# Windowed attention and a convolution gate: a woven order of work, two-bank and one-bank PSUM buffers, weights loaded later, half-size angle tables

## The chip, the core and the metric

The kernel runs on one core of a Trainium2 chip. The time is that of one execution on the device, in microseconds (us). TensorE (PE) has two clock levels, 1.2 and 2.4 GHz; the profile prints the granted clock as a share of the higher one, so 1.00 is 2.4 GHz and 0.50 is 1.2 GHz. DVE is VectorE, ACT is ScalarE, POOL is GpSimd, and SP issues most of the transfers (SPq is its queue of instructions).

## What is computed

The inputs are `q`, `k`, `v` of shape (4, 8, 768, 64), a flag per head, and the three weights of a gate, of shapes (512, 1536), (768, 512) and (512, 512). Of the reference, cut to what matters:

```python
scores = scale * np.matmul(q, k.transpose(0, 1, 3, 2))
stream_keep = causal & (is_sink | in_win)        # 4 sink keys, a window of 64
mask = np.where(retr, causal, stream_keep)       # per head
a = softmax(np.where(mask, scores, -1e9))
x = concat_heads(np.matmul(a, v))                # (4, 768, 512)
x1, x2, x3 = np.split(x @ w_proj, 3, axis=-1)
X2 = np.fft.rfft(x2, n=S, axis=1)
H = np.fft.rfft(filter_fft, n=S, axis=0)[None]
y = x1 * np.fft.irfft(X2 * H, n=S, axis=1) * x3
out = (y @ w_out).astype(np.float32)
```

## The kernel before

Work comes in 16 **pairs** (a batch and two heads, four pairs to a batch) and 4 **gates** (`moe`, one for each batch, which needs all four pairs of its batch).

A pair has these steps. `emit_loads` (L85) brings q, k and v in six transfers of 192 KB from SP's queue, two pairs ahead, into two sets of buffers. `emit_prep` (L224) casts them on DVE (L240, and L227 for `v_aug`), has POOL make `v_far`, the masked values, in four instructions (L233), turns q and k on PE (L243) and copies them out of PSUM on DVE (L245). `emit_scores` computes the scores in six chunks, each of up to four 128x128 blocks for both heads (`sc`, L258); ACT takes the exponential of each chunk (`pT`, L264), and DVE multiplies the blocks at the diagonal by the mask (L268 to L273). `emit_values` multiplies by the values, 42 small matmuls (`att`, L283), and DVE divides (L291, L293). `emit_turn` turns the result (L300) into `xT`.

A gate has five steps on PE: `x2` (24 matmuls of 512 columns, L314), `X`, the forward transform (12 full matmuls of 512 columns at L192 and 12 that fill half the columns of the array at L196), `x1p` and `x3p` (64 matmuls of 384 columns, L337 and L343), `ev` and `od`, the inverse transform (16 whole and 16 that use half the rows, L355 and L360), and `out_ps` (24 of 512 columns, L372). ACT copies each result out of PSUM one bank at a time (L317, L324, L340, L363, L375); DVE makes `P` (L326 to L329), `g` (L345), `conv` and `y` (L365 to L367). SP stores `o_sb`.

The transforms are matmuls with a table `G` of sines that the kernel computes first: DVE makes angles for 6 tiles of 128 (L168 to L172, three times) and ACT takes the sine (L174). `Gi` is `G` turned; `HA` and `HB` are the filter's transform (`emit_filter`, L205), which needs `filt`.

PSUM has eight banks: two buffers of two banks for the scores (`psw`), one of two banks for `att`, and two of one bank (`mps`) that everything else shares. The three weights are loaded from POOL's queue at the very start (L108, L110, L112).

The tile framework sets the order on each engine: it takes the order in which the code emits, and moves an instruction whose inputs are late behind others. The main loop (L383) emits a whole pair's scores, then the next pair's prep, then the pair's values, and after each pair one or two of the gate's five parts:

```python
        prep = preps.pop((b, hp))
        pT = emit_scores(hp, prep)
        if n + 1 < len(pairs):
            preps[pairs[n + 1]] = emit_prep(*pairs[n + 1])
        attn = emit_values(prep, pT)
        emit_turn(attn, xT, hp)
        next(gate, None)
```

## Time and profile before

| | us |
|---|---|
| median of 3 runs (328.66 to 329.56) | 329.06 |
| the profiled execution | 326.54 |
| its span, from the first to the last instruction | 324.8 |
| PE busy in the span | 240.5 (74%) |
| DVE busy | 183.8 (57%) |
| ACT busy | 157.1 (48%) |
| POOL busy | 42.2 (13%) |

PE's busy time counts matmuls that overlap once, but each with its way through the array, so a busy PE may still have room. No engine is busy for the whole span; which one sets the pace differs from stage to stage, so the page's shares say less than the same counts cut by stage.

### The profile page before, as it was taken

Reading aid. Unit: us, or ns where it says so; the run is one execution under the profiler, and the core shown is the slowest. Engines: PE = TensorE matmul, PEld = TensorE weight load, DVE = VectorE, ACT = ScalarE, POOL = GpSimd, SP = SyncE. Lnnn points to the kernel's source line nnn. Section 1 sums busy time; section 2 is a strip of 40 time slices with the busy share of each in tenths; the row PEclk is TensorE's granted clock in tenths of the full one; section 3 lists DMA queues with packets and bytes.
Section 4 is the critical chain, followed back from the end, with each engine's and each line's share of the span. In section 5 each row is a group of like instructions: output and inputs, shape, how many; then the busy total and the mean of one; then the engine's idle time right before and its main releaser. Section 6 shows DMA issues by size and latency. Waiting matters only on the chain.

```text
span 324.8 us, 4957 instructions
## 1 busy us (share of the span) xinstructions
PE 240.5 (74%) x1930; PEld 121.3 (37%) x1930; DVE 183.8 (57%) x353; ACT 157.1 (48%) x236; POOL 42.2 (13%) x97
## 2 busy tenths in 40 slices
...
GB/s 140 202 205 221 169 3 74 192 124 147 146 148 146 2 145 78 70 124 217 77 70 2 145 45 6 129 68 0 2 0 2 0 0 0 196 0 0 2 22 173
DMA packets 80727, 28.38 MB, mean 87 GB/s; under 512 B 75840, under 2 KB 77120, under 8 KB 80704
## 3 DMA queue, kind: packets, MB, share of 16 engines
q1 hardware_dynamic: 78864, 25.18, 35.1%
q0 software_dynamic: 1840, 2.88, 5.0%
...
## 4 chain that ended last, share of the span: by engine, by line
PE 46%; DVE 19%; ACT 16%; SPq 7%; DMA 7%; issue 5%; ACTq 0%; DVEq 0%
ACT pT L264 8%; PE x3p L343 7%; SPq L90 7%; PE x_ps L314 7%; DMA out_dram<-o_sb 5%; PE x1p L337 5%; PE att L283 5%; PE sc L258 4%; PE X_ps L192 3%; PE od L355 3%; ACT o_sb L375 2%; PE od L360 2%; DVE pT L270 2%; PE out_ps L372 2%; PE x_ps L300 2%
## 5 line engine op out<-in xcount | busy, mean ns | idle before, releaser
L264 ACT ACTIVATE pT<-sc 128x1024 bf16<-128x1024 f32 x96 | 82.4, 928 | 51.7 <-PE sc L258 51.7
L258 PE MATMUL sc<-qT,kT 64*128 64x512 bf16 (+3 forms) x256 | 40.2, 344 | 22.2 <-ACT pT L264 16.9
L283 PE MATMUL att<-v_aug,pT 128*128 128x65 bf16 x352 | 34.4, 210 | 8.3 <-DVE pT L270 4.8
L233 POOL TENSOR_SCALAR v_far<-v_aug,vmask 128x65 bf16<-128x65 bf16 (+1 forms) x64 | 34.2, 553 | 46.5 <-DVE vmask L144 25.8
L283 PEld LDWEIGHTS <-pT 128*128 128x128 bf16 x672 | 30.1, 109 | 16.9 <-DVE pT L270 7.8
L258 PEld LDWEIGHTS <-kT 64*128 64x128 bf16 x256 | 14.0, 98 | 44.4 <-issue 34.3
L372 PE MATMUL out_ps<-wout,y 128*128 128x512 bf16 x96 | 25.3, 399 | 6.2 <-ACT o_sb L375 5.3
L345 DVE TENSOR_TENSOR g<-x1s,x3p 128x384 bf16<-128x384 bf16 x32 | 17.7, 552 | 21.3 <-PE x3p L343 21.1
L270 DVE TENSOR_TENSOR pT<-pT,mask 128x1024 bf16<-128x1024 bf16 x32 | 22.0, 689 | 12.2 <-ACT pT L264 12.2
L340 ACT CAST x1s<-x1p 128x384 bf16<-128x384 f32 x32 | 15.3, 479 | 26.1 <-DVE g L345 16.8
L283 PE MATMUL att<-v_far,pT 128*128 128x65 bf16 x320 | 27.8, 211 | 0.0
L375 ACT COPY o_sb<-out_ps 128x512 f32<-128x512 f32 x24 | 13.6, 586 | 29.2 <-DMA out_dram<-o_sb 14.5
L343 PE MATMUL x3p<-xT,wproj 128*128 128x384 bf16 x128 | 26.1, 326 | 1.5 <-ACT x1s L340 0.8
L245 DVE COPY qT<-qT_ps 128x768 bf16<-128x768 bf16 x16 | 8.9, 554 | 30.9 <-PE qT_ps L243 30.9
L337 PE MATMUL x1p<-xT,wproj 128*128 128x384 bf16 x128 | 26.0, 325 | 0.0
L314 PE MATMUL x_ps<-wproj,xf 128*128 128x512 bf16 x96 | 21.6, 379 | 1.7 <-DVE kT L245 0.9
L363 ACT COPY evs<-ev 128x384 f32<-128x384 f32 x16 | 7.7, 481 | 29.9 <-PE ev L360 26.7
L243 PE MATMUL qT_ps<-identity,q_bf 128*128 128x128 bf16 x96 | 9.1, 236 | 16.4 <-DVE q_bf L240 9.7
L229 POOL MEMSET v_aug<- 128x12 bf16 x16 | 3.0, 192 | 139.7 <-PE att L283 139.7
L317 ACT CAST x<-x_ps 128x512 bf16<-128x512 f32 x24 | 14.1, 585 | 11.0 <-PE x_ps L314 11.0
L243 PE MATMUL kT_ps<-identity,k_bf 128*128 128x128 bf16 x96 | 9.8, 236 | 12.8 <-DVE k_bf L240 11.6
L326 DVE TENSOR_TENSOR m<-X,HA 128x1024 bf16<-128x1024 bf16 x12 | 8.2, 685 | 16.2 <-ACT X L324 16.2
...
## 6 DMA issues: line engine op xcount, KB each, us to landing
...
out_dram<-o_sb SPq DMA_DIRECT2D x24, 256.0 KB, 2.0
...
ret_i<-in_is_retrieval_dram SPq DMA_DIRECT2D x1, 8.0 KB, 3.6
```

The lines of the kernel that those rows point to most:

```text
L90: nc.sync.dma_start(out=t[:, :, 64 * hh:64 * hh + 64], in_=src[b, 2 * hp + hh].rearrange("(t p) d -> p t d", p=128))
L233: nc.gpsimd.tensor_scalar(out=v_far[:, j0:j1, hh, :], in0=v_aug[:, j0:j1, hh, :], scalar1=vmask[:, 2 * hp + hh, n:n + 1], scalar2=1.0, op0 ...
L243: nc.tensor.transpose(ps[:, t * 128:(t + 1) * 128], bf[:, t, :], identity)
L258: nc.tensor.matmul(sc[:, hh, n * 128:(n + cnt) * 128], lhsT=kT[rows, j * 128:(j + 1) * 128], rhs=qT[rows, i * 128:(i + cnt) * 128], start= ...
L264: nc.scalar.activation(out=pT[:, :, 512 * c:512 * c + w], in_=sc[:, :, 0:w], func=AF.Exp, scale=SCALE)
L270: nc.vector.tensor_mul(near[:, :, c:c + 2, 0:256], near[:, :, c:c + 2, 0:256], mask[:, h0:h0 + 2, 1, None, :].to_broadcast([128, 2, 2, 256]))
L283: nc.tensor.matmul(att[:, hh, 65 * i:65 * i + 65], lhsT=pT[:, hh, at:at + 128], rhs=(v_far if i >= j + 2 else v_aug)[:, j, hh, :], start=( ...
L314: nc.tensor.matmul(ps, lhsT=xf[:, cc, r, m * 128:(m + 1) * 128], rhs=wproj[:, cc, DM:2 * DM], start=(cc == 0), stop=(cc == NC - 1))
L337: nc.tensor.matmul(x1p, lhsT=wproj[:, cc, cb * 128:(cb + 1) * 128], rhs=xT[:, cc, cols], start=(cc == 0), stop=(cc == NC - 1))
L343: nc.tensor.matmul(x3p, lhsT=wproj[:, cc, 2 * DM + cb * 128:2 * DM + (cb + 1) * 128], rhs=xT[:, cc, cols], start=(cc == 0), stop=(cc == NC ...
L372: nc.tensor.matmul(ps, lhsT=y[:, cb, i * 128:(i + 1) * 128], rhs=wout[:, cb, :], start=(cb == 0), stop=(cb == NC - 1))
L375: nc.scalar.copy(out=o_sb, in_=ps)
```

## The change

The loop is written anew, and several tables and buffers with it.

- **Order.** A pair's six chunks are emitted one by one (`emit_chunk`). Behind chunks 0 and 1 come the two halves of the values of the pair before, behind chunk 1 the casts of the next pair, behind chunk 2 the turn of the pair before, behind chunk 3 the turning of the next pair's q and k, and behind chunks 0 to 4 one step of a gate. A gate now has 22 steps, each one tile of up to two banks: 3 of `x2`, 4 of `X`, 8 of `x13`, 4 of `c` (the inverse transform), 3 of `out`. A batch's gate begins behind chunk 2 of the next batch's first pair.
- **PSUM.** Three buffers of two banks (scores and gate tiles) and two of one bank (values, turns).
- **Copies.** ACT copies `x2`, `X`, `x1s` and `o_sb` with twice the width in half the instructions; stores are 512 KB. `v_aug` is cast on POOL, and `v_far` is one POOL instruction.
- **Transforms.** The mixed third tile of `X` is computed with full matmuls, and once more with its halves exchanged (24 full matmuls in place of 12 full and 12 half ones); the inverse takes 24 matmuls in place of 32.
- **Tables.** The angles are computed for 384 columns in place of 768, cosine and sine both from them; masks are made in bf16; the order of DVE and POOL in the setup is the code's own (`manual_schedule`).
- **Loads.** The flags and the first two pairs are loaded first. q, k and v take one transfer each (384 KB). Each weight's load is held until POOL has cast the values of pair 0, 1 or 2 (`hold`).

The diff, cut:

```diff
--- before.py
+++ after.py
...
-    psw = ctx.enter_context(tc.tile_pool(name="ps_w", bufs=2, space=bass.MemoryType.PSUM))
-    pso = ctx.enter_context(tc.tile_pool(name="ps_o", bufs=1, space=bass.MemoryType.PSUM))
-    mps = ctx.enter_context(tc.tile_pool(name="ps_m", bufs=2, space=bass.MemoryType.PSUM))
+    ps2 = ctx.enter_context(tc.tile_pool(name="ps2", bufs=3, space=bass.MemoryType.PSUM))
+    ps1 = ctx.enter_context(tc.tile_pool(name="ps1", bufs=2, space=bass.MemoryType.PSUM))
+
+    def bank_pair(name):
+        return ps2.tile([128, 2, 512], FP32, name=name, tag="w")
+
+    def bank(name, shape, dtype):
+        return ps1.tile(shape, dtype, name=name, tag="o")
...
+    ret_i64 = const.tile([128, H], mybir.dt.int64, name="ret_i64")
+    nc.sync.dma_start(out=ret_i64, in_=is_retrieval.partition_broadcast(128))
...
+        qk = ald.tile([128, 2, 2, NT, D], FP32, name="qk_f32")
+        vf = ald.tile([128, 2, NT, D], FP32, name="v_f32")
+        for dst, src in ((qk[:, 0], q), (qk[:, 1], k), (vf, v)):
+            nc.sync.dma_start(
+                out=dst, in_=src[b, 2 * hp:2 * hp + 2].rearrange("h (t p) d -> p h t d", p=128))
+        return qk, vf
...
+    loads = {pp: emit_loads(*pp) for pp in pairs[:1]}
+
+
+    setup_order = tc.manual_schedule(engines={mybir.EngineType.DVE, mybir.EngineType.Pool})
...
-    wproj = const.tile([128, NC, 3 * DM], BF16, name="wproj")
-    nc.gpsimd.dma_start(out=wproj, in_=moe_w_proj.rearrange("(c p) n -> p c n", p=128))
-    wout = const.tile([128, NC, DM], BF16, name="wout")
-    nc.gpsimd.dma_start(out=wout, in_=moe_w_out.rearrange("(c p) n -> p c n", p=128))
-    filt = setup.tile([128, NT, DM], BF16, name="filt")
-    nc.gpsimd.dma_start(out=filt, in_=moe_filter_fft.rearrange("(t p) c -> p t c", p=128))
...
+    turns = msb.tile([128, NM, HS], I32, name="turns", tag="P")
+    angle = msb.tile([128, NM, HS], FP32, name="angle", tag="g")
+    size = msb.tile([128, NM, HS], FP32, name="size", tag="y")
+    for m in range(NM):
+        nc.scalar.activation(out=turns[:, m], in_=fcol, func=AF.Copy, scale=tfrac[:, m:m + 1])
+    for m in range(NM):
+        nc.vector.tensor_scalar(out=angle[:, m], in0=fcol, scalar1=tcol[:, m:m + 1], scalar2=None,
+                                op0=ALU.mult)
+    for m in range(NM):
+        nc.vector.scalar_tensor_tensor(out=angle[:, m], in0=turns[:, m], scalar=-float(S),
+                                       in1=angle[:, m], op0=ALU.mult, op1=ALU.add)
+    nc.vector.tensor_scalar(out=size.bitcast(I32), in0=angle.bitcast(I32), scalar1=0x7fffffff,
+                            scalar2=None, op0=ALU.bitwise_and)
+    for out_, in_ in ((G[:, :, 0:4:2, :], size[:, :, 0:256]), (G[:, :, 4:6, 0:64], size[:, :, 256:384])):
+        nc.scalar.activation(out=out_, in_=in_.rearrange("p m (r f) -> p m r f", r=2), func=AF.Sin,
+                             scale=-ETA, bias=quarter)
+    for out_, in_ in ((G[:, :, 1:4:2, :], angle[:, :, 0:256]), (G[:, :, 4:6, 64:128], angle[:, :, 256:384])):
+        nc.scalar.activation(out=out_, in_=in_.rearrange("p m (r f) -> p m r f", r=2), func=AF.Sin,
+                             scale=-ETA)
...
-    for h in range(H):
-        nc.vector.scalar_tensor_tensor(
...
+    def emit_mask(engine, h):
+        engine.scalar_tensor_tensor(
...
-        e_t = setup.tile([128, 6, 128], FP32, name="e_t", bufs=2)
-        nc.vector.scalar_tensor_tensor(out=e_t, in0=fcol, scalar=tcol[:, m:m + 1], in1=off,
...
-        nc.vector.tensor_scalar(out=n_t, in0=e_t, scalar1=1.0 / S, scalar2=None, op0=ALU.mult)
-        nc.vector.scalar_tensor_tensor(out=e_t, in0=n_t, scalar=-float(S), in1=e_t,
-                                       op0=ALU.mult, op1=ALU.add)
-        nc.scalar.activation(out=G[:, m], in_=e_t, func=AF.Sin, scale=ETA)
...
+    def emit_matrix():
...
+        nc.gpsimd.tensor_copy(out=G[:, :, 6:8, 0:64], in_=G[:, :, 4:6, 64:128])
+        nc.gpsimd.tensor_copy(out=G[:, :, 6:8, 64:128], in_=G[:, :, 4:6, 0:64])
...
+    def emit_forward(src, tiles):
+
+        ps = bank_pair("X_ps")
+        for u, (t, r) in enumerate(tiles):
+            for m in range(NM):
+                nc.tensor.matmul(ps[:, u, :], lhsT=G[:, m, t, :], rhs=src[:, r, m, :],
+                                 start=(m == 0), stop=(m == NM - 1))
+        return ps
...
+        fold = msb.tile([128, 2, NM, DM], BF16, name="fold", tag="x2")
+        with tc.issue_after(state[3]["first"].ins):
+            nc.vector.tensor_add(fold[:, 0], filt[:, 0:NM, :], filt[:, NM:NT, :])
+            nc.vector.tensor_sub(fold[:, 1], filt[:, 0:NM, :], filt[:, NM:NT, :])
+
+        def put(out, in_, w):
+            nc.scalar.activation(out=out, in_=in_, func=AF.Copy, scale=w / S)
+
+        for t in range(2):
+            ps = emit_forward(fold, ((2 * t, t), (2 * t + 1, t)))
             for u in range(2):
-                nc.scalar.activation(out=HA[:, t, u, :], in_=re, func=AF.Copy, scale=2.0 / S)
+                put(HA[:, t, u, :], ps[:, 0, :], 2.0)
+                put(HB[:, t, u, :], ps[:, 1, :], 2.0 if u else -2.0)
...
+        plain = emit_forward(fold, ((4, 0), (5, 1)))
+        put(HA[0:64, 2, :, :], plain[0:64, :, :], 2.0)
+        put(HB[64:128, 2, :, :], plain[64:128, :, :], 2.0)
+        yield
+        swapped = emit_forward(fold, ((6, 0), (7, 1)))
+        put(HA[64:128, 2, :, :], swapped[64:128, :, :], 2.0)
+        put(HB[0:64, 2, :, :], swapped[0:64, :, :], -2.0)
+        yield
...
+    def emit_cast(st, a):
+        if a == 0:
+            st["bf"] = asb.tile([128, 2, NT, 2, D], BF16, name="qk_bf")
+        qk = loads[st["pair"]][0]
+        nc.vector.tensor_copy(out=st["bf"][:, a], in_=qk[:, a].rearrange("p hh t d -> p t hh d"))
...
+    def emit_v(st):
+        vf = loads.pop(st["pair"])[1]
+        st["v_aug"] = v_aug = asb.tile([128, NT, 2, 65], BF16, name="v_aug")
         nc.gpsimd.memset(v_aug[:, :, :, 64:65], 1.0)
...
-            for j0, j1, n in ((0, 1, 0), (1, 4, 1)):
-                nc.gpsimd.tensor_scalar(
...
+        nc.gpsimd.tensor_copy(out=v_aug[:, :, :, 0:64], in_=vf.rearrange("p hh t d -> p t hh d"))
+        st["v_far"] = v_far = asb.tile([128, 4, 2, 65], BF16, name="v_far")
+        hp = st["pair"][1]
+        nc.gpsimd.tensor_mul(v_far, v_aug[:, 0:4], vmask[:, hp, :, :, None].to_broadcast([128, 4, 2, 65]))
...
+    def emit_chunk(st, c):
...
+        sc = bank_pair("sc")
...
+        nc.scalar.activation(out=pT[:, :, 512 * c:512 * c + w], in_=sc[:, :, 0:w],
...
+    def emit_values(st, hh):
+        if hh == 0:
+            st["attn"] = asb.tile([128, NT, 2, 64], BF16, name="attn")
+        att = bank("att", [128, NT, 65], FP32)
...
-        for r in range(2):
-            for m in range(NM):
-                ps = mps.tile([128, DM], FP32, name="x2_ps", tag="m")
+        for m in range(NM):
+            ps = bank_pair("x2_ps")
+            for r in range(2):
...
+            nc.scalar.copy(out=x2[:, :, m, :], in_=ps)
+            yield
...
+            yield
...
+                ps = emit_forward(x2, ((6, 0), (7, 1)))
+                nc.scalar.copy(out=Xs, in_=ps)
+                yield
...
-        yield
...
-                x1p = mps.tile([128, HS], FP32, name="x1p", tag="m")
...
-                x3p = mps.tile([128, HS], FP32, name="x3p", tag="m")
...
-            if cb % 2:
-                yield
...
-            ev = mps.tile([128, HS], FP32, name="ev", tag="m")
-            od = mps.tile([128, HS], FP32, name="od", tag="m")
...
+            for part in (0, 2):
+                ps = bank_pair("x13_ps")
...
+                halves.append(ps[:, :, 0:HS])
+                if part == 0:
+                    x1s = msb2.tile([128, 2, HS], BF16, name="x1s")
+                    nc.scalar.copy(out=x1s, in_=halves[0])
+                    yield
+            nc.vector.tensor_mul(g[:, cb, :].rearrange("p (s t) -> p s t", s=2), x1s, halves[1])
...
+            ps = bank_pair("c_ps")
+            for r in range(2):
+                for n, (tile_no, t, u) in enumerate(((2 * r, r, 0), (2 * r + 1, r, 1), (4 + r, 2, r))):
+                    nc.tensor.matmul(ps[:, r, 0:HS], lhsT=P[:, t, u, ch], rhs=Gi[:, tile_no, :],
+                                     start=(n == 0), stop=(n == 2))
...
-        yield
-        for i in range(NT):
-            ps = mps.tile([128, DM], FP32, name="out_ps", tag="m")
...
+        for i in range(0, NT, 2):
+            ps = bank_pair("out_ps")
...
+            o_sb = msb2.tile([128, 2, DM], FP32, name="o_sb")
             nc.scalar.copy(out=o_sb, in_=ps)
-            nc.sync.dma_start(out=out[b, i * 128:(i + 1) * 128, :], in_=o_sb)
-        yield
-
-
-    preps = {pairs[0]: emit_prep(*pairs[0])}
-    gate = iter(())
+            nc.sync.dma_start(
+                out=out[b, i * 128:(i + 2) * 128, :].rearrange("(n p) c -> p n c", p=128), in_=o_sb)
+            yield
...
+    emit_cast(state[0], 0)
+    emit_mask(nc.vector, 0)
+    emit_mask(nc.vector, 1)
+    emit_cast(state[0], 1)
+    emit_prep(state[0])
+    emit_v(state[0])
+    setup_order.__exit__(None, None, None)
+    loads[pairs[1]] = emit_loads(*pairs[1])
...
+    def hold(first, n):
+
+        nc.gpsimd.tensor_copy(out=first, in_=state[n]["v_aug"][:, 0, 0, 0:1])
...
+        if b == 0 and hp + 1 < HP:
+            emit_mask(nc.vector, 2 * hp + 2)
+            emit_mask(nc.vector, 2 * hp + 3)
+        if n == 1:
+            emit_matrix()
+        if n == 2:
+            gates.append(setup_steps())
...
-        prep = preps.pop((b, hp))
-        pT = emit_scores(hp, prep)
-        if n + 1 < len(pairs):
-            preps[pairs[n + 1]] = emit_prep(*pairs[n + 1])
-        attn = emit_values(prep, pT)
-        emit_turn(attn, xT, hp)
-        if n == 0:
-            emit_inverse_matrix()
-        if n == 1:
-            emit_filter()
-        next(gate, None)
-        if hp % 2:
-            next(gate, None)
-        if hp == HP - 1:
-            for _ in gate:
-                pass
-            gate = moe(b, xT)
-    for _ in gate:
-        pass
+        st, last, nxt = state[n], state.get(n - 1), state.get(n + 1)
+        st["xT"] = xT
+        for c in range(len(CHUNKS)):
+            emit_chunk(st, c)
+            if c == 0 and last:
+                emit_values(last, 0)
+            if c == 1 and last:
+                emit_values(last, 1)
+            if c == (1 if n else 3) and nxt:
+                with tc.issue_after(st["first"].ins):
+                    for a in range(2):
+                        emit_cast(nxt, a)
+                emit_v(nxt)
+            if c == 2 and last:
+                emit_turn(last)
+                if hp == 0:
+                    gates.append(moe(b - 1, last["xT"]))
+            if c == (3 if n else 4) and nxt:
+                emit_prep(nxt)
+            if c == 4:
+                if n == 0:
+                    filt = msb.tile([128, NT, DM], BF16, name="filt", tag="xf")
+                    hold(filt[:, 0, 0:1], 0)
+                    nc.gpsimd.dma_start(out=filt, in_=moe_filter_fft.rearrange("(t p) c -> p t c", p=128))
+                if n == 1:
+                    hold(wproj[:, 0, 0:1], 1)
+                    nc.gpsimd.dma_start(out=wproj, in_=moe_w_proj.rearrange("(c p) n -> p c n", p=128))
+                if n == 2:
+                    hold(wout[:, 0, 0:1], 2)
+                    nc.gpsimd.dma_start(out=wout, in_=moe_w_out.rearrange("(c p) n -> p c n", p=128))
+            if c < 5:
+                gate_step()
...
+    emit_turn(last)
+    gates.append(moe(B - 1, xT))
```

How the instructions stand on three engines. On DVE, before, where the first masks and angles are made (`e_t` and `n_t` are angles, `kT` the turned keys of pairs 0 and 1):

```order
L245 COPY kT<-kT_ps 128x768
L115 TENSOR_SCALAR ret_w<-ret_i_108 128x16
L133 COPY stream<-causal 4x256
L118 TENSOR_TENSOR ret<-ret_w 128x8
L135 TENSOR_TENSOR only<-causal,stream 128x512
L144 COPY vmask<-ret 128x16
L168 SCALAR_TENSOR_TENSOR e_t<-fcol,tcol,off 128x768
L138 SCALAR_TENSOR_TENSOR mask<-only,ret,stream 128x512 x8
```

and after, the same place, up to the first mask multiply of pair 0 (L298):

```order
L159 TENSOR_SCALAR angle<-fcol,tcol 128x384 x3
L162 SCALAR_TENSOR_TENSOR angle<-turns,angle 128x384 x3
L164 TENSOR_SCALAR size<-angle 128x1152
L173 COPY stream<-causal 4x256
L175 TENSOR_TENSOR only<-causal,stream 128x512
L179 COPY vmask<-ret 128x32
L185 SCALAR_TENSOR_TENSOR mask<-only,ret,stream 128x512
L182 MEMSET vmask 4x4x2
L256 CAST qk_bf<-qk_f_81 128x768
```

The angles and one mask now stand ahead of the cast of the first queries; before, they stood behind the turned keys of the second pair.

On ACT, before, where the gate of the first batch ends and that of the second begins:

```order
L363 COPY evs<-ev 128x384 x2
L375 COPY o_sb<-out_ps 128x512 x6
L317 CAST x_1742<-x_ps 128x512 x6
L264 ACTIVATE pT<-sc 128x2x512 x5
L264 ACTIVATE pT<-sc 128x2x128
```

and after, the same place (numbers tell the buffers apart):

```order
L293 ACTIVATE pT_1400<-sc_1556 128x2x512
L405 COPY o_sb_1553<-out_ps_1544 128x1024
L344 CAST x2_1564<-x2_ps_1565 128x2x512
L293 ACTIVATE pT_1400<-sc_1575 128x2x128
L293 ACTIVATE pT_1585<-sc_1586 128x2x512
L344 CAST x2_1564<-x2_ps_1617 128x2x512
L293 ACTIVATE pT_1585<-sc_1627 128x2x512
L344 CAST x2_1564<-x2_ps_1666 128x2x512
```

The exponentials, which stood behind twelve copies of the gate in a row, now alternate with single copies of two banks.

On POOL, before, the first instructions behind the identity's memset:

```order
L108 DMA wproj<-in_moe_w_proj_dram 128x4x1536
L100 ISA
L100 AFFINE_SELECT identity<-identity 128x128
L110 DMA wout<-in_moe_w_out_dram 128x4x512
L112 DMA filt<-in_moe_filter_fft_dram 128x6x512
```

and after, behind the cast of the values of pair 0:

```order
L262 CAST v_aug<-v_f_82 128x12x64
L423 COPY filt<-v_aug 128x1
L471 DMA filt<-in_moe_filter_fft_dram 128x6x512
L195 TENSOR_SCALAR G<-par 128x3
L197 COPY G<-G 128x3x2x64
L265 TENSOR_TENSOR v_far<-v_aug,vmask 128x520
```

The filter's load now waits for the first values, and those of the other two weights for the values of pairs 1 and 2.

## Rows read from the trace of the kernel before

**Rows 1.** Stages: start:end, length, busy PE PEld DVE ACT POOL, granted clock, DMA share, GB/s.

```profile
0.00:29.30 29.30, 3.06 (x24) 2.02 (x24) 5.75 (x17) 1.28 (x1) 5.46 (x19) 1.00 1.02 187
29.30:80.50 51.20, 34.74 (x338) 21.55 (x335) 40.24 (x77) 32.12 (x43) 15.55 (x24) 0.87 0.68 127
80.50:253.50 173.00, 146.42 (x1309) 75.90 (x1305) 111.02 (x213) 101.78 (x151) 21.17 (x54) 0.99 0.34 76
253.50:281.80 28.30, 22.09 (x100) 7.29 (x101) 10.67 (x19) 5.18 (x11) 0.00 (x0) 0.64 0.10 38
281.80:324.80 43.00, 34.20 (x168) 14.50 (x167) 16.15 (x29) 16.76 (x31) 0.00 (x0) 0.98 0.13 49
```

**Rows 2.** Chain of waits in the first 40 us: start, length in us, what.

```profile
3.06 8.22 SPq L90
...
23.43 4.07 DMA k_f<-in_k_dram
...
33.06 5.58 DVE mask L138 x8
```

**Rows 3.** Waits over the span: us in total, times, longest.

```profile
ACT x1s L340 <- DVE g L345: 16.8, 14, 1.7
```

**Rows 4.** Timeline, PE and its weight loads (PEld), at granted clock 1.00.

```profile
55.40 0.61 PE L258 MATMUL sc<-qT,kT 64*128 64x512 bf16 x6 [0.65 <-DVE kT L245]
...
56.27 0.34 PEld L300 LDWEIGHTS <-attn 128*128 128x128 bf16 x6 [0.54 <-DVE attn L293]
...
281.79 5.34 PE L314 MATMUL x_ps<-wproj,xf 128*128 128x512 bf16 x24 [0.83 <-ACT o_sb L375]
```

**Rows 5.** Chain of waits: values at both clocks, and four matmuls of 384 columns.

```profile
69.77 2.15 PE att L283 x37
...
108.87 0.65 PE x1p L337 x4
...
126.62 1.31 PE att L283 x37
```

**Rows 6.** The page: DMA queues (packets, MB, share), issues (KB, us to landing).

```profile
q1 hardware_dynamic: 78864, 25.18, 35.1%
q0 software_dynamic: 1840, 2.88, 5.0%
...
out_dram<-o_sb SPq DMA_DIRECT2D x24, 256.0 KB, 2.0
...
ret_i<-in_is_retrieval_dram SPq DMA_DIRECT2D x1, 8.0 KB, 3.6
```

**Rows 7.** Groups by shape in the setup: busy us, mean ns, idle before.

```profile
L138 DVE SCALAR_TENSOR_TENSOR mask<-only,ret,stream 128x512 bf16<-128x512 f32 x8 | 5.7, 776 | 0.0
...
L172 DVE SCALAR_TENSOR_TENSOR e_t<-n_t,e_t 128x768 f32<-128x768 int32 x3 | 2.9, 957 | 0.0
...
L171 DVE TENSOR_SCALAR n_t<-e_t 128x768 int32<-128x768 f32 x3 | 1.9, 617 | 0.0
...
L128 POOL TENSOR_SCALAR_AFFINE_SELECT stream<-causal 128x512 f32<-128x512 f32 x1 | 0.6, 614 | 0.0
```

**Rows 8.** Instructions of one tile: duration in ns, least, median, most, first and last start.

```profile
L233 POOL TENSOR_SCALAR v_far<-v_aug,vmask x64: 316/438/1797, 32.3 to 229.0; 128x195 bf16<-128x195 bf16 x32, 128x65 bf16<-128x65 bf16 x32
...
L240 DVE CAST q_bf<-q_f x16: 547/550/604, 9.1 to 212.4; 128x768 bf16<-128x768 f32 x16
```

**Rows 9.** Timeline, ACT: start, us, operation, and idle time before it.

```profile
58.10 1.08 ACT L212 ACTIVATE HA<-X_ps 128x512 bf16<-128x512 f32 x2
...
80.53 4.96 ACT L264 ACTIVATE pT<-sc 128x1024 bf16<-128x1024 f32 x6 [3.82 <-PE sc L258]
```

**Rows 10.** As rows 1: the densest stretch of PE in the middle.

```profile
105.30:122.40 17.10, 15.70 (x138) 8.77 (x137) 12.60 (x25) 8.86 (x15) 2.17 (x5) 1.00 0.37 70
```

**Rows 11.** Timeline of the last gate: DVE on one quarter of the inverse, the last copies.

```profile
306.05 0.55 DVE L365 TENSOR_TENSOR conv<-evs,od 128x384 bf16<-128x384 f32 x1 [1.07 <-PE od L360]
306.52 0.55 DVE L366 TENSOR_TENSOR conv<-evs,od 128x384 bf16<-128x384 f32 x1
...
307.10 0.56 DVE L367 TENSOR_TENSOR y<-conv,g 128x768 bf16<-128x768 bf16 x1
...
320.30 1.24 ACT L375 COPY o_sb<-out_ps 128x512 f32<-128x512 f32 x2 [1.50 <-DMA out_dram<-o_sb]
```

303 lines of the change are left out of this document (131 added, 172 removed).

## The prediction

> **What bounds the kernel now.** The page's shares (PE 74%, DVE 57%, ACT 48%) name no bound, so I cut the span into stages and read the busy time of each [rows 1]. Five stand out. The **start**, 29.3 us to the first exponential, has every engine idle but the transfers: DMA share 1.02. The **first pairs** (pairs 0 to 3 and the filter, 51.2 us) have PE, DVE and ACT each at 60 to 80%, none full. The **middle** (173.0 us) holds pairs 4 to 15, two whole gates, and the third gate up to its `g`; PE is busy 85%, DVE 64%, ACT 59%. The **bridge** (28.3 us) ends the third gate, at a granted clock of 0.64. The **last gate** (43.0 us) stands alone. In the start, the chain of waits shows SP standing in one transfer's issue for 8.22 us and then k of the second pair still landing, 4.07 us [rows 2], while the three weights share the DMA. Behind that, eight masks in a row hold DVE for 5.58 us [rows 2], and the first values wait for them. In the middle, PE is busy but not dense, which the sum of the work shows below; one wait that tells why is ACT's for `g`, 16.8 us in 14 times [rows 3]: a shared one-bank buffer must be emptied before the next tile may be filled.
>
> **What PE's work is worth at the higher clock.** A chunk of scores adds 0.22 us (six matmuls, two chunks, take 0.61 us, of which I put 0.17 down to the way through the array) [rows 4]; a pair has 5.25, so 1.15. Values: 37 matmuls in 1.31 us, so 42 in 1.49 [rows 5]. Turns: 18 at 0.34 for six, 1.02 [rows 4]. A pair is 3.66 us. In a gate, 24 matmuls of 512 columns take 5.34 us [rows 4], and four of 384 take 0.65 [rows 5]. So `x2` 5.34, `X` (24 full after the change) 5.34, `x13` 16 times 0.65, 10.4, `c` (24) 3.9, `out` 5.34: 30.3 us. Before, `X` had twelve full and twelve half matmuls and `c` 32: about 29.2 by the same rates. The change hardly alters the work; it is the waits that can go.
>
> **Start: 29.3 to 14 us.** The weights' loads leave the start. Queue 1 moved 25.18 MB in 35.1% of 324.8 us, 0.22 MB per us [rows 6], so the first pair (1.18 MB) needs 5.3 us and is there at about 8. DVE's own chain then ends last. The flags take 3.6 us to land [rows 6], about 4.5. Then by halves of today's durations [rows 7]: three angle products 3 x 0.31, three corrections 3 x 0.48, `size` 0.9, `stream`, `only` and `vmask` about 1, a mask 0.78: 9.6. Then the casts of q and k (0.55 each, [rows 8]) with two masks between, 2.7: 12.3. Then k's turn, its copy and the first chunk, 0.8 + 0.55 + 0.6: 14.2. Ends: 10 if masks in bf16 cost half, 20 if the transfers are no faster than now. I take 14, since no row shows DVE slower than its own durations.
>
> **First pairs: 51.2 to 35 us.** Masks and angles lie ahead of them now. ACT's work is four times 4.96 us [rows 9] and nine-odd filter copies; two of 512 take 1.08 and follow each other at half of that [rows 9], which gives 8 copies 4.0 and five of double width 4.7: 28.5 in all. That is the low end. Above it: PE starts at the lower clock, where 37 values took 2.15 us against 1.31 [rows 5]; a pair's PE work is then 7.3 us, 2.3 over ACT's 5, for two pairs; and by pair 3 the DMA must have moved four pairs (21 us) and two weights beside them, of the 16 us that all three took (5.0% of the span, [rows 6]), some 2 us more than is hidden. 35; the high end is today's 51.
>
> **Middle: 173 to 143 us.** PE's work there is 12 x 3.66 + 3 x 30.3 less the third gate's `c` and `out` (9.2): 125.6 us. Today's is about 125 in 173.0, 72%. The densest stretch of today, 17.1 us [rows 10], holds 64 matmuls of 384 columns (10.4 us) and 74 of the pair's (about 3.3): 80%, with two one-bank buffers. After the change a tile of two banks is filled while two others are emptied, values and turns have buffers of their own, and the exponentials stand between single copies. I take 88%, between 80 and an end of 95: 143, with ends 157 and 132. The other engines stay below: DVE is busy 111.0 us there today [rows 1]; without twelve casts of `v_aug` (0.5 each) and with values divided in two halves (0.3 more a pair) it has some 108. ACT has 101.8 today, and less with its wider copies, about 96. DVE's cast of `v_aug` goes to POOL, idle for 88% of the middle [rows 1]; what is queued behind it there is `v_far`, and q, k and v loads two pairs later wait for it, with a pair's 12 us to spare.
>
> **Bridge: 28.3 to 16 us.** The last exponential, masks, second half of the values, division, turn: 3.2. The inverse goes at DVE's pace, 0.47 + 0.47 + 0.47 for each of four quarters [rows 11], and 1.2 ahead: 6.8. `out` 5.3 and a wait of 0.7. Today the same work ran at half the clock for the most part [rows 1]; ends 14 and 26.
>
> **Last gate: 43 to 40 us.** 5.3 + 1.3 (the last copy of `x2`) + 5.3 + 10.4 + 6.8 + 6.0, then the last copy 1.2 and a store of 512 KB, which for 256 KB took 2.0 [rows 6] and now perhaps 3. Ends 38 and 43.
>
> **Sum.** 14 + 35 + 143 + 16 + 40 = 248, against the span's 324.8. Outside the span lie 1.7 us (326.54 less 324.8): 249.7. The median of the runs stands 0.8% above the profiled execution (329.06 to 326.54): **252 us**, 241 to 264 with the middle between 85 and 93%.
>
> **Rivals.**
> *The weave keeps its waits.* Each engine is in order; a gate tile that waits on PE for its buffer now holds up scores and values too, which today stand in separate buffers. If the middle stays at today's 72%, it takes 174, +31: 283. For it: rows 3 show such waits; against: there are three buffers for what had two of half the size. 0.10.
> *POOL and DVE block each other.* POOL's `v_far` takes 316 ns at the least and up to 1797 [rows 8], long ones being at the setup beside DVE's two-input work; so something stretches it. After the change POOL casts 768 and multiplies 520 elements a pair: by 614 ns for 512 [rows 7] 1.5 us, twice that if both inputs count, and DVE might be kept out as long. DVE's middle would be 108 + 12 x 1.5 to 3.1, at 88% 143 to 165. I take +15: 267. Against: DVE's casts took 547 to 604 ns in all 16 pairs [rows 8], never stretched, with 1.75 us of POOL work a pair behind them. 0.09. The Trainium skill's page "SBUF — State Buffer", section "Who interferes with whom", states such a rule: VectorE and GpSimd share one pair of ports as an exclusive lock, and whichever issues second is fully blocked. By that rule this rival holds in full; the trace bears it out for POOL's side alone.
> *The clock falls in the bridge or stays low through pair 3.* DVE paces the inverse, so PE idles there, as it did when the clock fell to half before. `out` would take 10.4, and the filter's matmuls 5 more: +8, 260. 0.08.
> *Tighter.* The middle at 95% and the first pairs at ACT's 28.5: 235. 0.10.
> *The holds do nothing*, or the start is as slow for another reason: 14 becomes 29: 267. The order on POOL speaks against it. 0.02.
> *Slower.* Its mechanism is PE's clock: interleaved short tiles that never win the higher level. At 1.2 GHz throughout, the middle is 251 / 0.95 = 264, first pairs 45, bridge 23, last gate 70: 416. From 248 it is slower once 46% of that, 77 us, is lost, so if about half of PE's work runs at half clock. Against: the middle ran at 0.99 [rows 1] with more idle time. 0.03.
> Within 0.3%, about what a measurement can tell from no change here: 0.01, where losses happen to cancel.
>
> **How the numbers follow.** The forecast has 0.57, the rest as given. All but the last two are faster: 0.96, 0.01, 0.03. From 236 to 278 lie the forecast, the clock, the two of 267 and half of the tighter case: 0.81.
>
> **What would show it.** The first exponential at 14 us with no SP wait ahead of it; pair 4's first exponential near 49; pair 15's last near 192, and PE's idle time in between below 20 us, with no single waiter over 8; `conv` at DVE's pace without the clock at 0.50; the last `x2` starting near 208. If DVE's casts stretch beyond 0.6 us, the rival of the ports is right; if PE waits for exponentials or for `g` by tens of us, that of the waits. I am wrong altogether if the granted clock is at 0.50 for half of the middle.

## The result and the profile after

| | before | after |
|---|---|---|
| median | 329.31 us (4 runs, 328.66 to 331.88) | 260.26 us (4 runs, 259.99 to 260.79) |
| profiled execution, its span | 326.54, 324.8 | 259.99, 258.3 |

The ratio is 0.789, 95% interval 0.785 to 0.794. The forecast was 252 us, with a range of 236 to 278. So the sign and the size hold, and the time lies 8.3 us above the forecast. The stages tell where.

Profile of after, by stage, to be read against [rows 1] (start:end, length, busy PE PEld DVE ACT POOL, granted clock, DMA share, GB/s):

```profile
0.00:14.13 14.13, 2.29 (x18) 1.42 (x20) 10.75 (x26) 8.06 (x10) 7.00 (x22) 1.00 1.07 182
14.13:56.80 42.67, 28.62 (x310) 17.14 (x308) 28.89 (x55) 29.26 (x38) 13.69 (x18) 0.94 1.10 202
56.80:205.60 148.80, 141.82 (x1335) 73.67 (x1333) 113.62 (x221) 101.29 (x120) 22.90 (x33) 0.97 0.44 94
205.60:219.30 13.70, 12.19 (x83) 5.74 (x82) 10.45 (x21) 3.79 (x6) 0.00 (x0) 1.00 0.00 1
219.30:258.30 39.00, 30.91 (x161) 15.28 (x159) 15.18 (x25) 16.00 (x20) 0.00 (x0) 0.97 0.22 81
```

| stage | before | forecast | after |
|---|---|---|---|
| start, to the first exponential | 29.3 | 14 | 14.1 |
| first pairs, to pair 4's first exponential | 51.2 | 35 | 42.7 |
| middle, to pair 15's last exponential | 173.0 | 143 | 148.8 |
| bridge, to the last gate's `x2` | 28.3 | 16 | 13.7 |
| last gate | 43.0 | 40 | 39.0 |
| span | 324.8 | 248 | 258.3 |

Two stages miss: the first pairs by 7.7 us and the middle by 5.8. The last two give 3.3 back. Outside the span lie 1.7 us, as before. Some executions of the kernels below take 5 to 10 us longer, and the medians below leave them out (two expectations give e1 and e11 with them, up to 0.7 us higher); the profiled executions of e3, e8 and e11 are such ones, where k of the third or fourth pair lands about 5 us late, in e3 ahead of the stage that is read from it.

The chain of waits at the start, to be read against [rows 2] (start, length, what; L185 is the mask, L162 to L164 the angles, L298 pair 0's first mask multiply, L256 the cast):

```profile
0.81 3.15 DMA ret_i<-in_is_retrieval_dram
...
5.74 1.03 DVE angle L162 x2
...
9.32 1.97 DVE mask L185 x2
...
13.42 5.41 DVE mask L185 x4
18.84 0.33 DVE pT L298
19.17 0.56 DVE qk_bf L256
```

SP's 8.22 us and k's 4.07 us are gone, and behind the flags' transfer DVE's own work sets the start. But four masks in a row still hold DVE for 5.41 us, and they end 4.7 us after the first exponential has begun.

Of the waits over the span, the one for `g` [rows 3] has gone; ACT's copy of `x1s` waits for PE instead, and PE's scores wait a little for copies out of PSUM (us in total, times, longest):

```profile
ACT x1s L380 <- PE x_ps L373: 13.6, 12, 1.8
...
PE sc L287 <- ACT HB L231: 2.5, 3, 1.8
```

A shared buffer no longer holds anyone for long. The page's chain says what does, PE and DVE by turns:

```profile
PE 45%; DVE 37%; ACT 11%; issue 2%; DMA 2%; ACTq 0%
```

The transfers of the page answer to [rows 6]: queue 1 moves the same 25.18 MB in 46.1% of 258.3 us, 119 us against 114, and a store of 512 KB takes the 3 us that the forecast gave it.

```profile
q1 hardware_dynamic: 77904, 25.18, 46.1%
q0 software_dynamic: 1840, 2.88, 6.2%
...
out_dram<-o_sb SPq DMA_DIRECT2D x12, 512.0 KB, 3.1
```

### The profile page after: what moved, and what is told of

It reads as the page before. It is cut to its first block, busy times and chain, and to the rows that moved or that the text cites. A ratio compares the mean times of both kernels' runs of the same rounds, so it can differ in the third digit from the quotient of the medians.

```text
span 258.3 us, 4616 instructions
## 1 busy us (share of the span) xinstructions
PE 215.8 (84%) x1898; PEld 113.2 (44%) x1898; DVE 178.9 (69%) x346; ACT 158.4 (61%) x191; POOL 43.6 (17%) x72
## 3 DMA queue, kind: packets, MB, share of 16 engines
q1 hardware_dynamic: 77904, 25.18, 46.1%
## 4 chain that ended last, share of the span: by engine, by line
PE 45%; DVE 37%; ACT 11%; issue 2%; DMA 2%; ACTq 0%
PE x_ps L373 12%; PE x_ps L341 8%; PE att L313 6%; PE out_ps L402 5%; PE sc L287 5%; ACT pT L293 4%; DVE pT L300 4%; DVE qk_bf L256 4%; PE X_ps L207 3%; DVE y L396 3%; DVE mask L185 3%; DVE attn L321 3%; DVE conv L394 3%; DVE qkT L274 3%; PE qkT_ps L272 3%; DVE m L362 2%
## 5 line engine op out<-in xcount | busy, mean ns | idle before, releaser
L373 PE MATMUL x_ps<-xT,wproj 128*128 128x384 bf16 x256 | 46.7, 326 | 0.0
L287 PE MATMUL sc<-qkT 64*128 64x512 bf16 (+3 forms) x256 | 36.8, 331 | 4.7 <-ACT HB L231 2.5
L272 PE MATMUL qkT_ps<-identity,qk_bf 128*128 128x128 bf16 x192 | 16.8, 236 | 17.4 <-DVE qk_bf L256 14.9
L373 PEld LDWEIGHTS <-wproj 128*128 128x128 bf16 x256 | 23.3, 98 | 14.3 <-issue 1.3
L207 PE MATMUL X_ps<-x,G 128*128 128x512 bf16 x96 | 23.6, 379 | 0.5 <-ACT x L344 0.2
L341 PE MATMUL x_ps<-wproj,xf 128*128 128x512 bf16 x96 | 22.9, 383 | 0.3 <-DVE xf L334 0.3
L272 PEld LDWEIGHTS <-qk_bf 128*128 128x128 bf16 x192 | 12.8, 105 | 21.8 <-DVE qk_bf L256 15.7
L382 DVE TENSOR_TENSOR g<-x1s,x_ps 128x768 bf16<-128x768 bf16 x16 | 15.2, 950 | 8.6 <-PE x_ps L373 6.9
L256 DVE CAST qk_bf<-qk_f 128x768 bf16<-128x768 f32 x32 | 19.1, 608 | 0.2
L274 DVE COPY qkT<-qkT_ps 128x768 bf16<-128x768 bf16 x32 | 16.9, 548 | 2.9 <-PE qkT_ps L272 2.7
L265 POOL TENSOR_TENSOR v_far<-v_aug,vmask 128x520 bf16<-128x520 bf16 x16 | 18.5, 1158 | 1.2
```

Of the source, the lines that this page charges most:

```text
L207: nc.tensor.matmul(ps[:, u, :], lhsT=G[:, m, t, :], rhs=src[:, r, m, :], start=(m == 0), stop=(m == NM - 1))
L256: nc.vector.tensor_copy(out=st["bf"][:, a], in_=qk[:, a].rearrange("p hh t d -> p t hh d"))
L265: nc.gpsimd.tensor_mul(v_far, v_aug[:, 0:4], vmask[:, hp, :, :, None].to_broadcast([128, 4, 2, 65]))
L272: nc.tensor.transpose(ps[:, t * 128:(t + 1) * 128], st["bf"][:, a, t].rearrange("p hh d -> p (hh d)"), identity)
L274: nc.vector.tensor_copy(out=qkT[:, a], in_=ps)
L287: nc.tensor.matmul(sc[:, hh, n * 128:(n + cnt) * 128], lhsT=qkT[rows, 1, j * 128:(j + 1) * 128], rhs=qkT[rows, 0, i * 128:(i + cnt) * 128] ...
```

## The experiments

Twelve kernels, each the changed kernel with one edit unless said otherwise. Times are medians; on the chips of these runs the kernel before took 329.4 to 330.5 us, so they compare with 260.3 us within some 0.3%.

**e6: the weights' loads not held.**

```diff
+    nc.gpsimd.dma_start(out=filt, ...)      # first on POOL, and wproj, wout
...
-                    hold(wproj[:, 0, 0:1], 1)
```

> The three weights' loads are issued first thing on POOL, as before the change, and held by nothing; all else is as in the changed kernel. Theory (the loads beside the first pair's are what held the start): queue 0 takes 16 us of the 16 engines in all, so q, k and v of the first pair come up to 16 us later, the first exponential moves from 14.1 to 22-30 us, and since the same bytes no longer lie in the way of pairs 1 to 3, about half of that comes back: the whole 263 to 272 us. Rival (setup on DVE alone sets the start): first exponential at 14 to 16 us and the whole at 257 to 262 us.

Measured: 273.8 us (272.4 to 274.8), 13.5 more, above both ranges. The chain at the start, and the first two stages:

```profile
1.71 20.83 DMA qk_f<-in_k_dram
...
22.57 0.56 DVE qk_bf L260
```

```profile
0.00:25.43 25.43, 2.30 (x18) 1.43 (x20) 10.68 (x27) 8.06 (x11) 5.78 (x19) 1.00 1.01 181
25.43:70.90 45.47, 31.61 (x308) 18.51 (x308) 29.13 (x54) 29.30 (x38) 13.10 (x18) 0.92 0.79 145
```

k of the first pair takes 20.8 us from its issue. The start grows by 11.3 us, and nothing comes back later: the first pairs take 45.5 us though the weights are out of their way. The holds are worth 11.3 us of the start, where the forecast's rival had 15; that half would come back was wrong.

**e5: two buffers of two banks in PSUM in place of three. e4: the gate's steps not woven.**

```diff
-    ps2 = ctx.enter_context(tc.tile_pool(name="ps2", bufs=3, ...))
+    ps2 = ctx.enter_context(tc.tile_pool(name="ps2", bufs=2, ...))
```

```diff
-            if c < 5:
-                gate_step()
+            if c == 4:
+                for _ in range(5):
+                    gate_step()
```

> Two two-bank buffers in PSUM where the changed kernel has three; the two one-bank buffers stay. Theory (the third buffer is what lets PE fill while ACT and DVE empty two others, and was the larger part of the middle's gain): PE waits for ACT's and DVE's reads by 15 us or more, the middle goes from 148.7 to 158-170 us, the whole to 270 to 282 us. Rival (the buffers' width did it, since one copy takes what two took; the third is a spare): the whole stays at 260 to 264 us.

> The gate's steps are no longer set one behind each score chunk but five together behind the fifth chunk of a pair; buffers, loads and tables stay as in the changed kernel. Theory (the weave itself fills PE in the middle): PE waits for exponentials again as before the change, the middle goes from 148.7 to 160-172 us and the whole to 272 to 284 us. Rival (the two-bank buffers did it, the order matters little): the middle stays within 3 us and the whole at 259 to 264 us.

Measured: e5 285.9 us (283.3 to 286.4), more than its theory's 282 at the most; e4 269.8 us (268.3 to 271.0), between theory and rival. Their middles:

```profile
59.95:226.50 166.55, 147.45 (x1333) 77.37 (x1342) 115.34 (x221) 102.37 (x119) 23.44 (x33) 0.97 0.40 84
```

```profile
55.90:216.10 160.20, 142.63 (x1317) 81.42 (x1314) 115.72 (x222) 100.82 (x121) 23.94 (x33) 0.97 0.40 87
```

Without the third buffer the middle takes 166.6 us, 17.8 more, close to the 173.0 of before; the first pairs, bridge and last gate lose 3.1, 2.9 and 1.7 us too. Over e5's whole span PE's gate tiles wait some 18 us for ACT and DVE, which must first read a buffer (13 groups of waits, none over 3.3 us); in after such waits come to 0.9. So its theory holds. Without the weave it takes 160.2, 11.4 more, of which the shorter first pairs and bridge give 3.1 back. So of the two the third buffer is worth more, 25.6 us of the whole against 9.5. A bunched kernel with two buffers was not run.

**e3: POOL silent from pair 4 on. e2: POOL's `v_far` made twice.** In e3, `v_aug` and `v_far` of pair 3 serve for all later pairs.

```diff
+        if pairs.index(st["pair"]) > 3:
+            loads.pop(st["pair"])
+            st["v_aug"], st["v_far"] = v_aug_c, v_far_c
+            return
```

```diff
         nc.gpsimd.tensor_mul(v_far, v_aug[:, 0:4], vmask[...])
+        nc.gpsimd.tensor_mul(v_far, v_aug[:, 0:4], vmask[...])
```

> From pair 4 on POOL does nothing: v_aug and v_far of pair 3 are used again, v is loaded but not read, so the values of pairs 4 to 15 are wrong. Theory of the ports: DVE's busy time in the middle falls from 113.5 us by 6 to 12 us, its casts stay at 0.55 us, and the middle shortens from 148.7 to 140-145 us, the whole to 251 to 256 us. Rival (PE's and DVE's own work in turn set the middle's pace): DVE's busy time falls by less than 2 us and the time stays at 259 to 261 us.

> POOL multiplies v_far twice in each pair: 16 times 1.16 us, 18.5 us more POOL work, and nothing else changes. Theory of the ports (DVE is kept out while POOL works): DVE's busy time rises from 178.9 us by 6 to 18 us, its longest casts of q and k and its products stretch in the same places, and the time becomes 264 to 272 us. Rival (POOL and DVE work side by side; DVE's long instructions have another reason): POOL's busy time rises by 18.5 us, DVE's by less than 1 us, and the time stays at 259 to 261 us.

Measured: e3 255.9 us (255.5 to 257.3), e2 265.1 us (263.8 to 265.6), both at the near end of what the theory gave. e3's middle:

```profile
62.50:207.00 144.50, 141.53 (x1335) 73.91 (x1332) 108.02 (x222) 101.30 (x120) 0.00 (x0) 0.97 0.38 86
```

With POOL's 22.9 us gone, DVE's busy time falls by 5.6 us (113.62 to 108.02) and the middle by 4.3. In e2 POOL is busy 20.3 us more on the page (63.9 against 43.6), DVE 6.6 more (185.5 against 178.9), and the time rises by 4.8. So POOL's work costs DVE a quarter to a third of POOL's time. Where it is lost shows on one product. DVE and then POOL of after, in the same 3 us (start, us, what):

```profile
109.51 0.55 DVE L321 TENSOR_TENSOR attn<-att,rec 128x384 bf16<-128x384 f32 x1
109.97 0.54 DVE L395 TENSOR_TENSOR conv<-evs,c_ps 128x384 bf16<-128x384 f32 x1
...
110.55 1.26 DVE L396 TENSOR_TENSOR y<-conv,g 128x768 bf16<-128x768 bf16 x1
```

```profile
109.44 0.83 POOL L262 CAST v_aug<-v_f 128x768 bf16<-128x768 f32 x1
110.34 1.05 POOL L265 TENSOR_TENSOR v_far<-v_aug,vmask 128x520 bf16<-128x520 bf16 x1
```

and the least, median and most of `y` in ns, in after and in e3:

```profile
L396 DVE TENSOR_TENSOR y<-conv,g x16: 540/548/1372, 104.1 to 247.4; 128x768 bf16<-128x768 bf16 x16
```

```profile
L406 DVE TENSOR_TENSOR y<-conv,g x16: 545/548/559, 108.3 to 248.8; 128x768 bf16<-128x768 bf16 x16
```

`y`, which reads two tiles of SBUF, begins inside POOL's `v_far` and takes 0.7 us longer; `attn` and `conv`, which read one operand from PSUM, keep their 0.55 us beside POOL's cast, and never exceed 0.56 in the middle. The Trainium skill's page "SBUF — State Buffer", section "Who interferes with whom", says the same in its finer print: a DVE instruction with two SBUF inputs contends with a GpSimd instruction that reads SBUF, one with at most one SBUF input does not, unless it runs in a two-port mode. The trace agrees.

**e1 and e9: the masks of later pairs moved; then the weights' loads too.**

```diff
+            if c == (2 if n else 3) and b == 0 and hp + 1 < HP:
+                with tc.issue_after(st["first"].ins):
+                    emit_mask(nc.vector, 2 * hp + 2)
+                    emit_mask(nc.vector, 2 * hp + 3)
```

```diff
-                if n == 1:
-                    hold(wproj[:, 0, 0:1], 1)
+                if n == 2:
+                    hold(wproj[:, 0, 0:1], 2)
...
-                if n == 2:
-                    hold(wout[:, 0, 0:1], 2)
+                if n == 6:
+                    hold(wout[:, 0, 0:1], 6)
```

> The two masks of each later pair are made behind the running pair's first multiply instead of ahead of pair 0's. Theory (masks on DVE ahead of pair 0's first multiply, which starts at 18.84 us in the changed kernel, cost the first pairs time): the multiply starts near 13.5 us, pair 4's first exponential moves from about 56.9 to 53-55 us, and the whole takes 256 to 258 us. Rival (ACT's filter copies, 44 to 55.7 us, set the end of that stage whatever DVE does before): the multiply comes earlier all the same, but pair 4's first exponential stays within 1 us of 56.9 and the time within 259 to 261 us.

> As the kernel with the masks behind each pair's first multiply (267.6 us, k of pair 3 landed at 39.4 us after 10.1 us from its issue), but wproj's load is held for pair 2's v_aug and wout's for pair 6's instead of pairs 1's and 2's. Theory (the first pairs run at the DMA's limit: that kernel lost its 7 us because wproj's load shared the DMA with q and k of pair 3, which a changed order on SP put behind v): q and k of pair 3 land by 28 us, its first exponential comes near 38 us, pair 4's near 54, and the whole takes 254 to 258 us. Rival (the loss was DVE's new order or PE's lower clock): the whole stays at 264 to 268 us.

Measured: e1 266.9 us (266.1 to 268.3), 6.6 slower; e9 263.4 us (263.4 to 264.1). Both theories about e1 fell. The multiply does start at 14.6 us in place of 18.8, but e1's chain then stands on a transfer, and in e9 on masks again:

```profile
29.30 10.08 DMA qk_f<-in_k_dram
...
39.41 0.56 DVE qk_bf L256
```

```profile
26.85 1.33 DVE mask L185 x2
...
37.39 1.33 DVE mask L185 x2
```

In e1, SP's order changed with the DVE order: v of pair 3 went ahead of its q and k, and these met wproj's load. With the weights later that wait is gone and 3.5 us come back, less than e9's theory gave. The other 3.1 us remain: each pair's masks now stand ahead of the copies that the next pair needs, and PE's granted clock over these pairs is 0.84 against 0.94. Which of the two it is was not separated. The later masks of e9, as shown, take 1.33 us for two, where two of after's row of four took 2.7.

**e10: masks in two instructions. e12: that, the loads later, and the edits of e11 below.**

```diff
-        engine.scalar_tensor_tensor(out=mask[:, h], in0=only, scalar=ret[:, h:h + 1], in1=stream, ...)
+        engine.tensor_scalar(out=mask[:, h], in0=only, scalar1=ret[:, h:h + 1], ...)
+        engine.tensor_add(mask[:, h], mask[:, h], stream)
```

> Each mask is made in two instructions with two operands each (only by the flag, then plus stream) instead of one with three operands. Theory (DVE's work, 22.1 of the 25.9 us from 14.13 to 40 us, bounds pairs 0 to 2, and the masks' 9.0 us in eight are the part of it that can shrink): if a sum of 512 in bf16 takes what the first multiply of 512 does (0.33 to 0.41 us) and the product as much or less, a mask takes 0.5 to 0.75 us instead of 1.17, pair 0's first multiply starts 2 to 4 us sooner, and the whole takes 256 to 259 us. Rival (the transfers bound these pairs: 4 pairs of 5.5 us and 16 us of weights are 38 us): the multiply comes sooner, but pair 3's first exponential stays near 40 us and the whole at 259.5 to 261 us, or more if the loads' order changes.

Measured: 268.1 us (267.2 to 268.1), 7.8 slower, as the rival's last words allow. A mask whose two parts run undisturbed now takes 0.35 and 0.41 us, but some parts are stretched: one sum took 1.87 us beside POOL's `v_far` and a copy of POOL. So the eight masks take 8.9 us of DVE, no less than the 9.0 of after, and pair 0's first multiply starts at 18.5 us in place of 18.8, not 2 to 4 us sooner. The premise, cheaper masks, was not met:

```profile
12.68 1.87 DVE L187 TENSOR_TENSOR mask<-mask,stream 128x512 bf16<-128x512 bf16 x1
```

The loss is elsewhere; the chain goes through k of pair 2:

```profile
13.76 18.18 DMA qk_f<-in_k_dram
...
31.97 0.56 DVE qk_bf L255
```

POOL, whose own work beside these masks took less time, issued wproj's load at 17.2 us in place of 18.5; k, issued at 13.8 in both, landed at 31.9, where in after the second cast of that pair began at 26.45 and waited for nothing. e12 was made to test that:

> The kernel with the gate's steps mixed and HB's copies on DVE (253.9 us), with two changes more: masks in two instructions, which by themselves made the changed kernel 7.8 us slower (268.1 us, k of pair 2 landing at 31.9 us, 18.2 us after its issue), and wproj's load held for pair 2's v_aug, wout's for pair 6's. Theory (that loss was wproj's load, issued by POOL at 17.2 us, beside q and k of pairs 2 and 3 in the DMA; with wproj issued near 27 us it is gone and the cheaper masks show): k of pair 2 lands by 25 us, pair 3's first exponential comes at 36 to 39 us, and the whole takes 249 to 253 us. Rival (the two-step masks themselves are dear, by DVE's new order or PE's clock): the loss stays and the whole takes 257 to 262 us. Between the two, 253 to 257 us: wproj now lies in the way of pair 4's data instead, which k of pair 4 landing after 45 us would show.

Measured: 254.0 us (253.2 to 255.7, six runs). The first three stages:

```profile
0.00:16.04 16.04, 2.29 (x18) 1.42 (x20) 12.59 (x32) 8.06 (x10) 8.44 (x25) 1.00 1.06 176
16.04:53.18 37.14, 27.07 (x310) 15.93 (x309) 31.89 (x63) 25.55 (x32) 10.09 (x13) 1.00 1.16 211
53.18:199.80 146.62, 138.11 (x1307) 71.09 (x1318) 113.43 (x222) 100.49 (x119) 25.36 (x35) 0.99 0.47 99
```

DVE waits for no transfer in the first pairs any more; the loss of e10 is gone, so the weights' loads were its cause, wproj's at 17.2 us by the order of events (wout's, issued at 27.6 in e10, was moved with it). But against e11 (253.7) nothing is gained. The masks still take 8.8 us of DVE, and one sum of 1.8 us lies ahead of the last of the first turn's copies, so the start takes 16.0 us, as in e10. That wproj would now hold up pair 4, the expectation's reason for a time between 253 and 257, is not so either: k of pair 4 is cast at 43.4 us without a wait.

**e7: each quarter's inverse behind its own `x13`. e8: the filter's copies to `HB` on DVE. e11: both, and the products also in turn with `x13`.**

```diff
             nc.vector.tensor_mul(g[:, cb, :]..., x1s, halves[1])
             yield
-        for cb in range(NC):
-            ch = slice(cb * 128, (cb + 1) * 128)
             ps = bank_pair("c_ps")
```

```diff
+            if dve:
+                nc.vector.tensor_scalar(out=out, in0=in_, scalar1=w / S, scalar2=None, op0=ALU.mult)
+            else:
                 nc.scalar.activation(out=out, in_=in_, func=AF.Copy, scale=w / S)
```

```diff
+        for part in (product(0), gate13(0), product(1), gate13(1), product(2), gate13(2),
+                     inverse(0), inverse(1), gate13(3), inverse(2), inverse(3)):
+            yield from part
```

> Each quarter's inverse (c, conv, y) follows its own x13 tiles and g, where the changed kernel makes all four quarters' x13 first. No work changes. Theory (in the middle PE and DVE take turns as the bound, because the gate's steps that are long on PE stand together and those that are long on DVE too: the chain holds DVE for 9.6 us at 102.2 and for 11.2 us at 155.3): the middle goes from 148.7 to 140-146 us and the last gate, where the inverse runs at DVE's pace alone, from 38.9 to 33-36 us: the whole 248 to 255 us. Rival (each engine's own total sets the pace, whatever the order): the middle stays within 2 us, the last gate alone gains, 255 to 259 us.

> The filter's copies to HB (4 of 512 columns, 2 of 1024) are made by DVE instead of ACT. Theory (in pair 3 the filter's copies and the exponentials stand in a row on ACT, 44.0 to 56.6 us, while DVE is busy 3.3 us of the 10 from 50 to 60): pair 4's first exponential moves from 56.9 to 52-54 us and the whole to 255 to 258 us. Rival (what comes next, the data of pair 4 or wproj by DMA, or PE at the lower clock, is late anyway): pair 4's first exponential stays after 55.5 us and the whole at 259 to 261 us.

> The gate's steps are mixed further than in the kernel with x13 and inverse in turn (256.6 us): forward tiles with their products also alternate with the x13 quarters; and the filter's copies to HB are made by DVE, which alone gave 257.1 us. Theory (both gains are real and lie in different stages, 3.6 and 3.1 us, and the products' stretch of DVE, 128.8 to 138.2 us in the kernel with x13 and inverse in turn, is the next of the same kind): 249 to 253 us. Rival (the middle has no slack left beyond those two, PE's own work sets it): 253 to 254.5 us; or the products now come late for the inverse and PE waits, 255 us or more.

Measured: e7 256.6 us (256.1 to 256.9), e8 257.1 (257.1 to 257.1), e11 253.7 (253.5 to 254.0). e7's last three stages:

```profile
56.45:203.65 147.20, 139.85 (x1320) 72.91 (x1328) 115.40 (x226) 100.97 (x121) 23.61 (x33) 0.97 0.46 95
203.65:216.50 12.85, 12.05 (x86) 6.37 (x86) 8.61 (x16) 3.61 (x6) 0.00 (x0) 1.00 0.00 0
216.50:254.80 38.30, 30.28 (x159) 15.36 (x159) 15.67 (x25) 16.02 (x20) 0.00 (x0) 0.94 0.23 83
```

The middle gains 1.6 us, the bridge 0.9, the last gate 0.7. The middle and the whole are the rival's, but its reason, that the last gate alone gains, is not what happened. PE's timeline of the last gate says why the gain is small there. In after (first fence), the inverse's 24 matmuls ran in 4.06 us of the time in which DVE set the pace; in e7 (second) they stand between `x13` tiles, so PE's work takes the place of DVE's:

```profile
230.07 10.56 PE L373 MATMUL x_ps<-xT,wproj 128*128 128x384 bf16 x64
240.47 4.06 PE L389 MATMUL c_ps<-Gi,P 128*128 128x384 bf16 x24
...
247.01 4.52 PE L402 MATMUL out_ps<-wout,y 128*128 128x512 bf16 x20 [0.33 <-DVE y L396]
```

```profile
227.29 2.76 PE L373 MATMUL x_ps<-xT,wproj 128*128 128x384 bf16 x16
...
244.03 4.06 PE L400 MATMUL out_ps<-wout,y 128*128 128x512 bf16 x18 [0.37 <-DVE conv L393]
```

From `x13`'s first matmul to the dense part of `out` pass 16.9 us in after and 16.7 in e7. e8's 3.1 us are within what the theory gave for ACT's row of filter copies in pair 3; its stage can't be read, since in its profile k of the fourth pair is late. The gains of e7 and e8, 3.6 and 3.1, add up in e11 (6.5); the products' place adds nothing to be seen. e11 and e12 are the fastest kernels of the study: 0.772 (0.766 to 0.778) and 0.770 (0.766 to 0.773) of the time before. The transforms, ACT's wider copies and the smaller tables had no run of their own.

## Why the prediction was right where it was, and where it failed

- **Start, 14: right, for the reason given.** The first exponential comes at 14.13 us with no SP wait ahead of it; without the holds it comes at 25.4. That the holds do nothing is refuted.
- **First pairs, 35 against 42.7: the step that failed is "Masks and angles lie ahead of them now".** By the diff two of eight masks are made in the setup and six in the loop, and after's chain has four in a row that end at 18.8 us. With that step went a whole engine: the sum took ACT's work (28.5 forecast, 29.3 measured, right) and then PE and DMA, but not DVE, which [rows 1] showed busy longest of all in that stage. DVE is busy 22.1 us of the first 25.9 (the three stretches below); there the chain stands on DVE for some 12 us and on PE for 10. From 44.0 to 56.6 us it stands on ACT's filter copies and exponentials, the bound that the forecast took for the whole stage; e8, which takes `HB` from that row, is 3.1 us faster. How much of the miss is the masks' is not shown, since no kernel made them cheaper or gained by moving them. In e12 pair 4's first exponential came at 53.2 us, where the forecast had 49 and after 56.8; but e8's edit, which e12 has too, was alone worth 3.1 us of the whole.

```profile
14.13:20.00 5.87, 1.65 (x13) 0.51 (x9) 5.87 (x7) 3.77 (x4) 4.84 (x6) 1.00 1.25 209
20.00:30.00 10.00, 7.92 (x97) 5.20 (x96) 8.21 (x17) 6.58 (x8) 3.91 (x5) 1.00 1.15 220
30.00:40.00 10.00, 8.18 (x105) 5.63 (x105) 8.05 (x19) 5.18 (x6) 1.32 (x3) 0.83 1.24 232
```

- **The rest of the 35.** Of the 6.6 us that the forecast added to ACT's work, the 4.6 for a lower clock did not come as such: the clock is 1.00 up to 30 us and 0.83 in the ten behind. The "some 2 us more than is hidden" for the transfers stand nowhere on after's chain in this stage, though the DMA share is 1.10; they are near, for e1, e10 and e6 each stand on k for 10 to 21 us after its issue.
- **A mask was priced at 0.78 [rows 7]; it took 0.74 at the least and 1.17 on average.** The four in a row took 5.49 us while POOL was busy 5.0 us of that time; in e6, with little more than one cast on POOL beside them, four took 3.30 (DVE and POOL in after, then DVE in e6). So the rival of the ports, read below from the middle, has some 3 us of DVE's time here too, an estimate from eight times 1.17 less 0.74.

```profile
13.35 5.49 DVE L185 SCALAR_TENSOR_TENSOR mask<-only,ret,stream 128x512 bf16<-128x512 bf16 x4
```

```profile
13.45 1.04 POOL L265 TENSOR_TENSOR v_far<-v_aug,vmask 128x520 bf16<-128x520 bf16 x1
...
16.25 1.37 POOL L265 TENSOR_TENSOR v_far<-v_aug,vmask 128x520 bf16<-128x520 bf16 x1
```

```profile
24.64 3.30 DVE L191 SCALAR_TENSOR_TENSOR mask<-only,ret,stream 128x512 bf16<-128x512 bf16 x4
```

- **Middle, 143 against 148.8: the mechanism right, one term too good.** 125.6 us of PE's work in 148.8 is 84%, where I took 88, a choice between 80 and 95 with no row of its own. e3 shows 4.3 of the 5.8 us: with POOL silent it is 87%, and DVE's busy time is 108.0, the forecast's 108, in place of 113.6. Most of the miss is thus the rival of the ports, which I had as a case apart instead of as a term. ACT's wider copies saved nothing to be seen, 101.3 against 96 forecast and 101.8 before. The rest is the turns that PE and DVE take in the chain; e7 got 1.6 of it.
- **The rival of the ports: real, and oversized.** I gave it 1.5 to 3.1 us a pair by letting POOL stop DVE for its whole length, +15 in all. It costs 0.47 us of DVE a pair (5.6 over 12), 4.3 us of time. By the sign that the prediction named, casts beyond 0.6 us, it is there: the argument against it was casts that never stretched [rows 8], but in after's middle some take 1.13 us, and in e3's none over 0.56. `attn`, read from PSUM, keeps its time (least, median, most in ns):

```profile
L256 DVE CAST qk_bf<-qk_f x20: 516/552/1127, 74.0 to 187.2; 128x768 bf16<-128x768 f32 x20
L321 DVE TENSOR_TENSOR attn<-att,rec x22: 542/548/558, 73.2 to 197.9; 128x384 bf16<-128x384 f32 x22
```

- **The weave keeps its waits (283): the mechanism exists, two buffers bring it (e5, 285.9), three don't.** The reason that spoke against it, three buffers for two of half the size, holds.
- **Bridge and last gate: 13.7 and 39.0 against 16 and 40.** The bridge lies below its low end of 14: the forecast set values, turn, inverse and `out` one behind the other, but in after the values and the turn lie between the gate's steps, and 9 of `out`'s 24 matmuls run before the inverse's last `y`. The last gate's terms add up to 39.3, nearer than the 40 written. The rival that the clock falls in the bridge was wrong: it is 1.00 there (and its two losses, 5.1 and 5, make 10, not 8).
- **Tighter (235) and slower:** the first pairs went at ACT's pace in their last third alone, and the granted clock stays at 0.97 in the middle.
- The step from the profiled execution to the median, 0.8% or 2 us, was not there after the change (259.99 and 260.26), so the span's sum missed by 10.3 us and the time by 8.3. That this covered 2 us of the miss is luck. A middle at 85 to 93% gives 244 to 257 us by the forecast's own sum, which does not hold the time; the 241 to 264 written beside it does.
